# Pairing heads h and h+6 in a score unit, all remaps on SyncE, and a two-queue model of the transfers in the planner

## Chip, cores and metric

The kernel runs on one core of a Trainium2 chip. The metric is the device time of one execution in microseconds (us), given as the median over the runs. The profile is of one execution of its own, and all rows below come from that one.

The core has five instruction streams that matter here. TensorE (PE) multiplies matrices. VectorE (DVE), ScalarE (ACT) and GpSimd (POOL) work on tiles in the on-chip buffers, and GpSimd can also issue transfers. SyncE (SP) computes nothing; it issues transfers, in the order in which the program gives them to it. Each stream works strictly in its own order, so an instruction that waits holds back everything behind it on that engine. The transfers are carried by 16 DMA engines.

## The reference, cut

Talking-heads attention (the heads are mixed before and behind the softmax) feeds two feed-forward blocks.

```python
# q, k, v: [4 batches, 12 heads, 448 positions, 64]; w_pre, w_post: [12, 12]
s = np.matmul(q, k.transpose(0, 1, 3, 2)) / 8
s = np.einsum('bhij,hg->bgij', s, w_pre)
a = np.exp(s - max(s, -1)); a = a / (sum(a, -1) + 1e-9)
a = np.einsum('bhij,hg->bgij', a, w_post)
x = np.matmul(a, v)                      # -> [1792, 768]
h = x @ w_in                             # 768 -> 2048 (weights in float64)
g = where(h >= 1, h, where(h <= -1, 0, (h + 1)**2 / 4))
x = g @ w_out                            # 2048 -> 768
h = x @ w_in2                            # 768 -> 1024
y = h * softmax(h); y = layernorm(y) * g_ln
out = y @ w_out2                         # 1024 -> 768
```

## The kernel before, in words

**Chunks.** Attention is the first third of the program (to about 360 us), and the change is all in it. It runs over 16 chunks: four batches of 448 query positions, each cut into chunks of 110, 110, 110 and 120 positions (`GR` = 11, 11, 11, 12 groups of `R` = 10). Nothing is kept between the chunks but the keys and values of a batch.

**From queries to mixed scores.** For each chunk `load_q` brings the queries of all heads into one of two buffers `qb`. It loads two half tiles; in each the 64 rows are the head's dimensions and a row holds six pieces, one for each head. For each batch `load_k` brings the keys, one tile `kraw` for two heads (ten buffers). A score unit `qk` is four matmuls for two neighbouring heads, 2p and 2p+1, whose queries lie in the lower and the upper 64 partitions; it fills two PSUM tiles of [query position, 448]. `qk_evac` scales and copies each to a tile `s` (12 buffers) on ScalarE; for the odd heads of chunk 0, VectorE does it. Then a transfer, `remap`, moves each `s` tile (110 or 120 rows of 1792 bytes) into the score buffer `sr`. It has two buffers, for even and odd chunks. In `sr` a partition is one head of one position, so that the mixing of heads is a matmul. There are twelve remaps for a chunk. SyncE issues them, but for six of chunk 0 that GpSimd issues.

**From mixed scores to output.** The groups of a chunk are taken two at a time (90 pairs in all). `pre` is eight matmuls that mix the heads, from `sr` with the small weight `wp`. `rmax` (VectorE) finds the row maximum, `expo` (ScalarE) the exponential and its sum, `guard` (GpSimd) and `norm` (VectorE) the reciprocal, `wscale` (GpSimd) multiplies it into the second mixing weight. `post` is 56 small matmuls, `evac` (ScalarE, VectorE) copies into `at`, `av` multiplies by the values, and `store_x` writes the rows of x to memory. The first `pre` of a chunk needs all twelve remaps of the chunk, and the first remap of a chunk needs the last `pre` of the chunk two before it, since that has the same score buffer.

**Near weights.** Beside this, four blocks of the float64 weights of the first feed-forward block are loaded (`e_load`, into `eraw`, one buffer, 0.79 MB each) and taken apart on VectorE, ScalarE and GpSimd (`e_exp` at line 481, `e_pow` at 484 and what follows) into float32, which `e_stash` writes back. They are numbered n = 0 to 3 here; two come from `w_in`, two from `w_out`.

**What sets the order.** A planner (`Order`) places all instructions of all engines before the program is built. Each task has an engine, an estimated duration, its dependences, rings (a pool of n buffers, of which a task takes or frees one) and a priority, which is its place in units of groups with an offset from the table `OFFS`. `emit` always takes the task that can start first, and among those of one engine the one of lowest priority. A transfer is two tasks (`dma`): its issue on an engine, and its flight, which takes a fixed time `xfer` for that kind of load plus 950 ns, whatever else is in flight. A list `gates` holds a load's issue back, in the plan, until the `pre` of a given group. The planner's times only make the order; on the chip each engine waits for the real events.

At the start of the program (`start` in `OFFS`) the first keys and the first queries are loaded in small steps, so that the first two heads can begin early. VectorE clears four rows of the first score buffer (`zero_s`), GpSimd clears small tiles (`zero_w`) and loads the two mixing weights in eight small transfers (`load_w`), from which VectorE forms `wp` and `wk` (`make_w`).

## Time and profile before

| what | value |
|---|---|
| runs before (us) | 1060.23, 1062.01, 1070.85; median 1062.01 |
| span of the profiled execution (us) | 1064.1 |
| TensorE busy | 1016.8 us, 96% of the span, mean granted clock near full |
| VectorE busy | 740.7 us, 70% |
| ScalarE busy | 621.7 us, 58% |
| GpSimd busy | 352.1 us, 33% |
| transfers | 171.41 MB in 101422 packets, mean 161 GB/s |

A row of the timeline reads: start, duration, engine, line and operation, output and inputs with their shape, "x" and the number of instructions in the row, and in brackets how long the engine stood idle before it and what ended that. "SPq" is the issue of transfers on SyncE. In the table by stage, each row is a stretch of the span, and for each engine the busy time and, as "x", the number of instructions. PEld is the loading of weights into TensorE, which lies beside the matmuls. PEclk is the clock that TensorE was granted, as a share of full speed. The last two columns are the mean busy share of the 16 DMA engines and what they moved.

### The profile page before, as it was taken

To read this page: it belongs to the slowest core of one execution; us is meant where nothing else is said; L and a number is where in the kernel's file an instruction comes from. 1 tells how busy PE (TensorE), PEld (TensorE's weight loads), DVE (VectorE), ACT (ScalarE), POOL (GpSimd) and SP (SyncE) were. 2 spreads that over 40 slices of the span, in tenths; PEclk is the share of its full clock that TensorE was granted. 3 is DMA by queue.
4 is the path that set the end of the run, shared out by engine and by line. 5 is a ranking of instruction groups with operands and counts; after the bars stand their busy time and mean duration, and the time that the engine had idled before them with its cause. 6 is when DMAs were issued, how large, how long until landed. Compare 5 with 4: busy or idle time off the path is not lost.

```text
span 1064.1 us, 27355 instructions
## 1 busy us (share of the span) xinstructions
PE 1016.8 (96%) x11053; PEld 836.5 (79%) x11053; DVE 740.7 (70%) x1259; ACT 621.7 (58%) x1329; POOL 352.1 (33%) x475
## 2 busy tenths in 40 slices
PE   6869987999999899999999999999999999999998
PEld 2435655665666589999999999999998878889998
DVE  4535654555556763489897768888887899888782
ACT  3666966778878665633444434343434577686770
POOL 3111321211111341445454555464521245041210
PEclk9999999999999999999999999999999999999999
DMA  8766787477575460242424232423355556697421
GB/s 182 204 176 171 205 264 196 141 218 218 176 219 196 155 204 17 79 139 70 139 99 131 98 118 74 148 92 119 124 183 184 195 179 227 232 332 239 159 79 60
DMA packets 101422, 171.41 MB, mean 161 GB/s; under 512 B 22752, under 2 KB 77888, under 8 KB 101296
## 3 DMA queue, kind: packets, MB, share of 16 engines
q1 hardware_dynamic: 100560, 168.46, 50.6%
q0 software_dynamic: 736, 1.21, 0.6%
q8 instruction: 87, 1.43, 0.6%
q14 instruction: 39, 0.32, 0.1%
HBM read 91.07 MB, written 39.85 MB: 123 GB/s over the span
## 4 chain that ended last, share of the span: by engine, by line
PE 80%; DMA 10%; DVE 4%; ACT 3%; issue 1%; SPq 1%; POOL 1%; ACTq 0%; DVEq 0%
PE ps_h L820 7%; PE ps_o L850 7%; PE ps_h L822 7%; PE ps_o L852 7%; PE ps_h L821 7%; PE ps_o L851 7%; PE ps_pre L340 6%; PE ps_post L376 5%; PE ps_av L427 4%; PE ps_qk L313 4%; DMA sr<-s 4%; PE ps_ot L1184 3%; PE ps_ot L1186 3%; PE ps_ot L1185 3%; PE ps_h L1184 3%; PE ps_h L1186 3%
## 5 line engine op out<-in xcount | busy, mean ns | idle before, releaser
L345 DVE TENSOR_REDUCE nm<-ps_pre 128x1 f32<-128x448 f32 x180 | 105.8, 617 | 50.7 <-PE ps_pre L340 43.0
L850 PE MATMUL ps_o<-g,wout 128*128 128x448 f32 x384 | 139.5, 363 | 0.9 <-DVE x2acc L860 0.9
L852 PE MATMUL ps_o<-g,wout 128*128 128x448 f32 x384 | 139.1, 362 | 0.0
L851 PE MATMUL ps_o<-g,wout 128*128 128x448 f32 x384 | 138.4, 360 | 0.0
L376 PEld LDWEIGHTS ps_post<-wr,p 64*64 64x64 f32 x5040 | 103.1, 136 | 41.2 <-issue 24.7
L350 ACT ACTIVATE p<-ps_pre,nm 128x448 f32<-128x448 f32 x180 | 114.2, 642 | 24.1 <-DVE nm L345 23.9
L842 POOL TENSOR_TENSOR g<-t,g 128x448 fp32r<-128x448 f32 x64 | 83.4, 1303 | 108.5 <-ACT g L838 96.1
L340 PE MATMUL ps_pre<-sr,wp 64*64 64x448 f32 (+1 forms) x720 | 104.8, 575 | 13.6 <-DMA sr<-s 4.0
L313 PE MATMUL ps_qk<-kraw,qb 64*64 64x448 f32 (+2 forms) x768 | 102.8, 568 | 15.1 <-DMA qb<-in_q_dram 5.8
L324 ACT ACTIVATE s<-ps_qk 119x448 f32<-119x448 f32 (+1 forms) x186 | 92.6, 568 | 38.8 <-PE ps_qk L313 24.7
L860 DVE TENSOR_TENSOR x2acc<-ps_o,x2acc 128x448 f32<-128x448 f32 x168 | 100.4, 617 | 19.5 <-PE ps_o L852 18.1
L739 POOL TENSOR_TENSOR m<-m,v 128x768 f32<-128x768 f32 (+1 forms) x48 | 88.6, 1847 | 71.2 <-DVE v L721 56.3
L376 PE MATMUL ps_post<-wr,p 64*64 64x60 f32 x5040 | 104.5, 221 | 4.8 <-issue 2.2
L357 POOL TENSOR_SCALAR nm<-nm 128x2 f32<-128x2 f32 x90 | 19.2, 213 | 235.6 <-ACT p L350 235.5
L826 ACT ACTIVATE t<-ps_h,st 128x448 f32<-128x448 f32 x64 | 40.4, 631 | 69.4 <-PE ps_h L822 67.7
L711 ACT ACTIVATE v<-v,st 128x768 int32<-128x768 int32 (+1 forms) x48 | 42.3, 880 | 64.1 <-DVE v L707 64.0
L852 PEld LDWEIGHTS ps_o<-g,wout 128*128 128x128 f32 x384 | 72.1, 188 | 5.6
L850 PEld LDWEIGHTS ps_o<-g,wout 128*128 128x128 f32 x384 | 72.1, 188 | 5.1 <-DVE x2acc L860 1.3
L340 PEld LDWEIGHTS ps_pre<-sr,wp 64*64 64x64 f32 (+1 forms) x720 | 30.4, 135 | 58.0 <-issue 16.7
L851 PEld LDWEIGHTS ps_o<-g,wout 128*128 128x128 f32 x384 | 71.8, 187 | 5.0
L820 PE MATMUL ps_h<-sr,win 128*128 128x448 f32 x192 | 70.3, 366 | 0.0
L427 PE MATMUL ps_av<-at,vv 128*64 128x240 f32 (+1 forms) x648 | 68.3, 353 | 1.5 <-issue 1.5
(192 smaller groups left out, 2434.1 us busy)
## 6 DMA issues: line engine op xcount, KB each, us to landing
sr<-s SPq DMA_DIRECT2D x138, 192.5 KB
raw<-in_moe_w_out_dram SPq DMA_DIRECT2D x22, 768.0 KB
raw<-in_moe_w_in_dram SPq DMA_DIRECT2D x14, 768.0 KB
sr<-s SPq DMA_DIRECT2D x48, 210.0 KB
xe<-e SPq DMA_DIRECT2D x14, 512.0 KB
el<-xe SPq DMA_DIRECT2D x14, 512.0 KB
raw<-in_moe_w_in_dram SPq DMA_DIRECT2D x12, 512.0 KB
kraw<-in_k_dram SPq DMA_DIRECT2D x24, 224.0 KB
```

Source lines behind the costliest of these rows:

```text
L313: nc.tensor.matmul(out=qk_t[b, c, 2 * p + e][64 * j:at_], lhsT=qb[rows, i % 2, lo:hi], rhs=kraw_t[b, p][rows], start=True, stop=True,)
L324: nc.scalar.activation(out=s[:n], in_=qk_t.pop((b, c, h))[:n], func=AF.Copy, scale=0.125)
L340: nc.tensor.matmul(out=pre_t[t][o:o + 64], lhsT=wp[k_], rhs=sr[i % 2][k_, g, :], start=True, stop=True)
L345: nc.vector.tensor_reduce(nm_t[t // 2][:, 0, t % 2:t % 2 + 1], pre_t[t], axis=AX.X, op=ALU.max, negate=True)
L350: nc.scalar.activation(out=p, in_=pre_t.pop(t), func=AF.Exp, bias=nm[:, 0, e], accum_out=nm[:, 1, e])
L376: nc.tensor.matmul(out=ps[i][64 * j:64 * j + 64, k, :], lhsT=ps_p[e][64 * i:64 * i + 64, x:x + 64], rhs=wr[64 * i:64 * i + 64, e], start=T ...
L427: nc.tensor.matmul(out=ps[0][64 * j:64 * j + 64, a, :2 * w].rearrange("p (e s c) -> p e s c", e=2, c=SEG), lhsT=v_t[b][:, 1 + m, h * D:(h ...
L820: nc.tensor.matmul(out=ps, lhsT=wh, rhs=xh, start=(kk == 0), stop=False)
L850: nc.tensor.matmul(out=ps, lhsT=wh, rhs=g[:, 0], start=(i == 0), stop=False)
L851: nc.tensor.matmul(out=ps, lhsT=wh, rhs=g[:, 1], start=False, stop=False)
L852: nc.tensor.matmul(out=ps, lhsT=wl, rhs=g[:, 0], start=False, stop=(i == 1))
L860: nc.vector.tensor_tensor(out=dst, in0=op.pop((u, m)), in1=dst, op=ALU.add)
```

## The change

- A score unit now holds heads p and p+6 (in `qk`, and in the loads). The lower 64 partitions hold heads 0 to 5, the upper ones heads 6 to 11. So a query load is two transfers of 64 rows, each one piece of 2640 bytes (2880 in a chunk of 120), where each row had six pieces of 440 bytes; and the first query load of the program is no longer split.
- A key load is now for four heads (two units), in two halves of 64 partitions with two pieces each. The bytes are the same, and there are five buffers of double size for ten.
- All remaps are issued by SyncE. The six of chunk 0 that GpSimd issued are gone from there. `zero_s(0)` goes from VectorE to GpSimd.
- In the planner, the flight of a transfer now queues: `give` keeps two "wires", and each kind of load takes time on one or both of them (`XFER`), then `LAND`. A remap takes 88 ns for each group on the first wire alone.
- The query load of chunk 1 is held in the plan until eight remaps of chunk 0 are issued (`hold`), that of chunk 2 until the first `pre`. The near loads move earlier by four groups (`pr - 8` for `pr - 4`).

The diff, cut to these parts (the long lines of the start tuple and of the old chunk loop are left out):

```diff
+   mw=-5, hold=8, q2=0)
...
+BUFS = dict(kraw=5, q=2, vv=2, s=12, sr=2, p=8, st=8, wr=6, x=3, psa=4, psb=4)
...
+LAND = 1300
+XFER = dict(load_k=lambda *a: (1240, 1240), load_q=lambda *a: (1000, 1000), load_v=lambda *a: (1700, 1000),
+            remap=lambda i, b, c, h, e: ((88 if e == 'SP' else 150) * GR[c], 0), e_load=lambda n: (4000, 3000), e_stash=lambda n: (1700, 1000),
+            store_x=lambda *a: (1000, 900))
...
-        d = self.add("DMA", xfer, prio, nothing, deps=[t], use=on, lat=950)
+        d = self.add("DMA", 0, prio, nothing, deps=[t], use=on, lat=LAND)
         d.issue = t
+        d.load = XFER.get(fn.__name__, lambda *a: (xfer, xfer))(*a)
...
+    def give(self, t, latency, avail, wire, done):
+        for o in t.out:
+            o.ready = max(o.ready, t.start + t.dur + latency(t, o))
+            o.left -= 1
+            if not o.left:
+                if o.eng == 'DMA':
+                    wire[:] = [max(w, o.ready) + x if x else w for w, x in zip(wire, o.load)]
+                    o.start = o.ready
+                    o.dur = max(w for w, x in zip(wire, o.load) if x) - o.ready
+                    done.append(o)
+                    for r, k in o.gives:
+                        r.open_[k] -= 1
+                        if not r.open_[k]:
+                            r.back.append(k)
+                    self.give(o, latency, avail, wire, done)
+                else:
+                    avail[o.eng].append(o)
...
-        nc.vector.memset(sr[i][0:pad], 0.0)
+        (nc.vector if i else nc.gpsimd).memset(sr[i][0:pad], 0.0)
...
     def load_k(b, p):
-        t = pl['kraw'].tile([128, S], F32, tag="kraw", name="kraw")
-        nc.sync.dma_start(out=t, in_=k[b, p])
-        kraw_t[b, p] = t
-
-    def load_q(i, b, c, p0, n):
-        m = GR[c] * R
-        qp = q[b, c, :, :H * m].rearrange("d (p e m) -> e d p m", e=2, m=m)
+        t = pl['kraw'].tile([128, 2, S], F32, tag="kraw", name="kraw")
+        heads = k[b].rearrange("p (e d) s -> d (p e) s", e=2)
         for e in range(2):
-            nc.sync.dma_start(
-                out=qb[e * D:(e + 1) * D, i % 2, QPAD + p0 * m:QPAD + (p0 + n) * m].rearrange("d (p m) -> d p m", m=m),
-                in_=qp[e, :, p0:p0 + n],
-            )
+            nc.sync.dma_start(out=t[e * D:(e + 1) * D], in_=heads[:, 6 * e + p:6 * e + p + 2])
+        kraw_t[b, p], kraw_t[b, p + 1] = t[:, 0], t[:, 1]
+
+    def load_q(i, b, c):
+        n = H // 2 * GR[c] * R
+        for e in range(2):
+            nc.sync.dma_start(out=qb[e * D:(e + 1) * D, i % 2, QPAD:QPAD + n], in_=q[b, c, :, e * n:(e + 1) * n])
...
+        for h in (p, p + 6):
...
-        x = od.dma("SP", 450, 2200, pr - 4, e_load, n, new=[r_er])
-        gates.append((x, pr - 4))
+        x = od.dma("SP", 450, 2200, pr - 8, e_load, n, new=[r_er])
+        gates.append((x, pr - 8))
...
-    t_z = add("Pool", 600, -100, zero_w)
-    t_zs = [add("DVE", 5700, -120, zero_s, 0)]
-    t_lw = add("Pool", 8000, P['lw'], load_w, deps=[t_z], lat=2500)
+    t_z = add("Pool", 1700, -1000, zero_w)
+    t_lw = add("Pool", 5000, P['lw'], load_w, deps=[t_z], lat=3500)
     t_w = add("DVE", 300, P['mw'], make_w, deps=[t_lw])
+    t_zs = [add("Pool", 5700, P['lw'] + 1, zero_s, 0)]
...
+        if i:
+            pr = t0 + P['sq'] - 3
+            q0 = od.dma("SP", 1250, 2000, pr, load_q, i, b, c, new=[r_q], deps=held if i == 1 else ())
+            gates.append((q0, pr if i > 2 else P['q2'] if i == 2 else -1))
+        for p in range(H // 2):
+            pr = t0 + P['qk0'] + P['qks'] * 2 * p
+            if c == 0 and p % 2 == 0:
+                kt[b, p // 2] = od.dma("SP", 900, 1240, pr + P['sk'] - 2 if b else -100, load_k, b, p, new=[r_kraw])
+                if b:
+                    gates.append((kt[b, p // 2], pr + P['sk'] - 2))
+                if i == 0 and p == 0:
+                    q0 = od.dma("SP", 1250, 2000, -100, load_q, i, b, c, new=[r_q])
+            a1 = add("PE", 754, pr, qk, i, b, c, p, deps=[q0, kt[b, p // 2]], new=[r_psa, r_psa],
+                     use=[(r_q, i), (r_kraw, b * H // 4 + p // 2)])
+            for e in range(2):
+                h = p + 6 * e
+                en, dur = ("DVE", 550) if i == 0 and e else ("Activation", 470)
+                a2 = add(en, dur, pr + P['qks'] * e, qk_evac, b, c, h, en, deps=[a1], new=[r_s], use=[(r_psa, -1 if e else -2)])
+                rms.append(od.dma("SP", 850, 900, pr + P['qks'] * e, remap, i, b, c, h, "SP", deps=[a2], use=[(r_s, -1)],
+                                  new=[] if rms else [r_sr], join=[r_sr] if rms else []))
+                if i == 0 and len(rms) == P['hold']:
+                    held = [rms[-1].issue]
```

The planner decides the order from these numbers, so here is what it puts where, at three places.

SyncE's queue from the start of the program, before (`kraw` are keys, `qb` queries, `sr<-s` remaps of 11 groups; "x" counts like transfers in a row):

```order
L282 DMA kraw<-in_k_dram 128x448
L289 DMA qb<-in_q_dram 64x110 x2
L282 DMA kraw<-in_k_dram 128x448
L289 DMA qb<-in_q_dram 64x2x110 x2
L282 DMA kraw<-in_k_dram 128x448 x2
L289 DMA qb<-in_q_dram 64x3x110 x2
L282 DMA kraw<-in_k_dram 128x448 x2
L289 DMA qb<-in_q_dram 64x6x110 x2
L329 DMA sr<-s 10x11x448 x6
L289 DMA qb<-in_q_dram 64x6x110 x2
L329 DMA sr<-s 10x11x448 x11
```

And of the change:

```order
L304 DMA kraw<-in_k_dram 64x2x448 x2
L310 DMA qb<-in_q_dram 64x660 x2
L304 DMA kraw<-in_k_dram 64x2x448 x4
L347 DMA sr<-s 10x11x448 x9
L310 DMA qb<-in_q_dram 64x660 x2
L347 DMA sr<-s 10x11x448 x6
L310 DMA qb<-in_q_dram 64x660 x2
L347 DMA sr<-s 10x11x448 x6
L320 DMA vv<-in_v_dram 64x768 x2
L347 DMA sr<-s 10x11x448 x3
```

Six remaps on SyncE stood between the last piece of query load 0 and query load 1, beside six on GpSimd, and the eleven behind that load were of chunk 1. Now nine stand ahead of query load 1, the last three of chunk 0 and three of chunk 1 behind it, and query load 2 comes before the other remaps of chunk 1.

SyncE's queue around the near load n=3, before (`eraw` is that load; remaps of 12 groups are those of chunk 7, those of 11 groups behind it are of chunk 8):

```order
L282 DMA kraw<-in_k_dram 128x448 x4
L329 DMA sr<-s 10x12x448 x6
L282 DMA kraw<-in_k_dram 128x448
L329 DMA sr<-s 10x12x448 x2
L282 DMA kraw<-in_k_dram 128x448
L329 DMA sr<-s 10x12x448 x4
L473 DMA eraw<-in_moe_w_out_dram 128x1536
L289 DMA qb<-in_q_dram 64x6x110 x2
L329 DMA sr<-s 10x11x448 x4
```

And of the change (`xs<-x` is the store of finished rows):

```order
L310 DMA qb<-in_q_dram 64x660 x2
L478 DMA xs<-x 128x2x228
L304 DMA kraw<-in_k_dram 64x2x448 x2
L478 DMA xs<-x 128x2x228
L304 DMA kraw<-in_k_dram 64x2x448 x2
L491 DMA eraw<-in_moe_w_out_dram 128x1536
L347 DMA sr<-s 10x12x448 x6
L304 DMA kraw<-in_k_dram 64x2x448 x2
L347 DMA sr<-s 10x12x448 x6
```

The near load stood behind all twelve remaps of chunk 7 and all six key loads of the next batch; now it stands before those remaps and the last key load.

TensorE's order around the first `pre`, before; the numbers tell tiles apart, four `qk` rows are one unit, and 44 rows of `qk` stand ahead of these, so the first unit here is the twelfth, the last of chunk 1:

```order
L313 MATMUL ps_qk_287<-kraw_169,qb_117 64x448
L313 MATMUL ps_qk_287<-kraw_169,qb_117 55x448
L313 MATMUL ps_qk_288<-kraw_169,qb_117 64x448
L313 MATMUL ps_qk_288<-kraw_169,qb_117 55x448
L340 MATMUL ps_pre_302<-sr_119,wp_115 64x448 x2
L340 MATMUL ps_pre_303<-sr_119,wp_115 64x448 x2
L340 MATMUL ps_pre_311<-sr_119,wp_115 64x448 x2
L340 MATMUL ps_pre_312<-sr_119,wp_115 64x448 x2
L313 MATMUL ps_qk_326<-kraw_129,qb_117 64x448
L313 MATMUL ps_qk_326<-kraw_129,qb_117 55x448
L313 MATMUL ps_qk_327<-kraw_129,qb_117 64x448
L313 MATMUL ps_qk_327<-kraw_129,qb_117 55x448
```

And of the change; 32 rows of `qk` stand ahead of these, so the first unit here is the ninth:

```order
L331 MATMUL ps_qk_244<-kraw_134,qb_117 64x448
L331 MATMUL ps_qk_244<-kraw_134,qb_117 55x448
L331 MATMUL ps_qk_245<-kraw_134,qb_117 64x448
L331 MATMUL ps_qk_245<-kraw_134,qb_117 55x448
L358 MATMUL ps_pre_253<-sr_119,wp_115 64x448 x2
L358 MATMUL ps_pre_254<-sr_119,wp_115 64x448 x2
L331 MATMUL ps_qk_264<-kraw_134,qb_117 64x448
L331 MATMUL ps_qk_264<-kraw_134,qb_117 55x448
L331 MATMUL ps_qk_265<-kraw_134,qb_117 64x448
L331 MATMUL ps_qk_265<-kraw_134,qb_117 55x448
```

All twelve units of chunks 0 and 1 stood before the first `pre`, and chunk 2's first units came behind two of them. Now nine stand before it, three of them of chunk 1, and the other three of chunk 1 come between the next ones.

## Rows read from the trace of the kernel before

**Rows 1.** Table by stage, core 0; PEclk is the granted clock (share).

```profile
core 0: us, PE busy (x) PEld busy (x) DVE busy (x) ACT busy (x) POOL busy (x), PEclk, DMA share, GB/s
0.00:28.20 28.20, 17.46 (x99) 5.50 (x99) 12.94 (x10) 10.14 (x19) 9.69 (x24) 0.94 0.83 181
28.20:46.00 17.80, 14.54 (x308) 7.96 (x309) 9.22 (x20) 13.07 (x35) 2.89 (x10) 0.91 0.79 221
46.00:69.40 23.40, 18.49 (x380) 9.56 (x381) 10.15 (x22) 16.57 (x43) 3.44 (x12) 1.00 0.65 177
69.40:84.00 14.60, 10.30 (x218) 5.92 (x218) 7.07 (x14) 6.63 (x17) 2.53 (x6) 0.88 0.64 171
...
134.00:147.00 13.00, 10.57 (x270) 7.08 (x264) 6.80 (x17) 7.91 (x24) 2.97 (x6) 1.00 0.87 270
...
172.00:186.00 14.00, 7.69 (x174) 5.35 (x174) 4.80 (x13) 5.65 (x16) 2.16 (x5) 0.96 0.84 200
186.00:344.00 158.00, 154.01 (x3683) 98.51 (x3683) 89.44 (x213) 128.08 (x365) 28.61 (x93) 0.99 0.66 193
344.00:376.00 32.00, 27.41 (x707) 19.43 (x703) 25.93 (x54) 22.06 (x56) 10.29 (x18) 0.95 0.58 189
376.00:800.00 424.00, 424.00 (x2247) 396.23 (x2238) 321.46 (x447) 185.12 (x297) 204.53 (x153) 1.00 0.35 113
```

**Rows 2.** Timeline of TensorE: first "pre" of chunks 0, 1, 2.

```profile
28.19 1.76 PE L340 MATMUL ps_pre<-sr,wp 64*64 64x448 f32 x6 [1.90 <-DMA sr<-s]
...
46.00 0.59 PE L340 MATMUL ps_pre<-sr,wp 64*64 64x448 f32 x2 [2.73 <-DMA vv<-in_v_dram]
...
69.41 0.98 PE L340 MATMUL ps_pre<-sr,wp 64*64 64x448 f32 x8 [2.11 <-DMA sr<-s]
```

**Rows 3.** Chain of waits: start, us, what.

```profile
44.32 11.09 DMA sr<-s
...
129.17 4.83 DMA sr<-s
...
172.04 10.97 DMA eraw<-in_moe_w_out_dram
```

**Rows 4.** Timeline, 169 to 187 us, VectorE and TensorE.

```profile
183.04 0.56 DVE L481 TENSOR_SCALAR ev<-eraw 128x768 int32<-128x768 int32 x1 [8.30 <-DMA eraw<-in_moe_w_out_dram]
...
184.66 0.81 PE L418 MATMUL ps_av<-at,vv 64*64 64x120 f32 x14 [4.81 <-ACT ev L484]
```

**Rows 5.** DMA view, 60 to 65 us: packets, MB, share of 16 engines.

```profile
DMA packets 1103, 0.74 MB, mean 148 GB/s; under 512 B 764, under 2 KB 1103, under 8 KB 1103
...
q1 hardware_dynamic: 1103, 0.74, 63.6%
```

**Rows 6.** DMA view, 120 to 125 us.

```profile
q1 hardware_dynamic: 585, 0.97, 60.9%
```

**Rows 7.** Timeline of SyncE's queue: remaps issued, start us, us.

```profile
9.35 7.36 SPq L329 DMA_DIRECT2D sr<-s  x6
...
18.36 14.92 SPq L329 DMA_DIRECT2D sr<-s  x11
...
43.36 15.14 SPq L329 DMA_DIRECT2D sr<-s  x12
...
117.13 10.19 SPq L329 DMA_DIRECT2D sr<-s  x11
...
159.80 5.17 SPq L329 DMA_DIRECT2D sr<-s  x6
```

**Rows 8.** Line 329, the remaps, over the whole span.

```profile
L329 SPq DMA_DIRECT2D sr<-s x186: 755/756/2167, 9.4 to 335.4; - x186
...
DMA to landing us min/median/max: 5.8/8.7/10.0
```

**Rows 9.** Timeline of GpSimd and VectorE, 0 to 16 us.

```profile
0.98 0.83 POOL L251 MEMSET at<- 128x840 f32 x1
...
1.90 4.54 DVE L254 MEMSET sr<- 4x5376 f32 x1 [1.90 <-issue]
```

## The prediction

> **What bounds it now.** I read the table by stage first, with edges where the trace shows a chunk's first "pre" matmul [rows 1]. From 376 us on TensorE has hardly a gap (424.00 of 424 us busy to 800), so whatever attention loses is lost at the end. From 186 to 344 it is 97% busy and runs 3683 instructions in 158 us, 23.3 per us; I use that as its full pace. From 28.2 to 84 it runs only 308 + 380 + 218 = 906, worth 39 us at that pace, in 55.8 us: 17 us are lost. From 172 to 186 it runs 174, worth 7.5 us of 14: 6.5 lost. From 134 to 147 it runs 270, worth 11.6 of 13: 1.4 lost. Before 28.2 it runs 99 "qk" instructions and waits for loads.

> The timeline then says who was late. Each chunk's first "pre" needs all twelve remaps of its chunk, and the waits of TensorE at 28.19 and 69.41 end in a remap, that at 46.00 in the load beside the last one [rows 2]. The chain of waits has a single remap at 11.09 us from issue to landing where it ends at ScalarE [rows 3]. ScalarE works in order, so an evacuation that waits for a buffer still held by such a remap holds the exponentials behind it. The second kind of stall is the near-weight load eraw: it is issued at 172.04 and on the chain for 10.97 us [rows 3], VectorE waits 8.30 us for it, and TensorE's gap of 4.81 us ends with the step of ScalarE behind that [rows 4].

> **The change, part by part.** *Query loads.* In a window that holds one query load, 1103 packets took 63.6% of 16 engines in 5 us, 50.9 engine-us; 764 of them are its 440-byte pieces, the 339 others hold the other 0.40 MB [rows 5]. In a window of remaps alone 585 packets took 60.9%, 48.7 engine-us, about 87 ns for a row of 1792 bytes [rows 6]; scaled by bytes the 339 took 20 engine-us, so a small piece costs 40 ns. A query load is 768 pieces, 1.9 us on each engine; after, 128 rows of 2640 bytes, by bytes 128 ns each: 1.0 us. It saves 0.9 us a chunk. From 186 us on TensorE's 97% hides that; at the start it is inside the sums below.

> *Remaps: what paces them.* SyncE issued eleven back to back in 10.19 us, 0.93 each, where issuing one takes 0.756 [rows 7, 8]. While it did, the engines were 60.9% busy and no other load was queued [rows 6], so the transfers set the pace, with six engines' worth idle. The rows fit a remap that uses ten engines: 110 rows of 87 ns over ten are 0.96 us, over sixteen 0.60. [...] I take the row. So one queue of ten engines, not SyncE, carries the start, and the planner's two classes describe what the trace shows.

> *All remaps of chunk 0 on SyncE.* Six leave GpSimd, whose remaps landed 8.7 us after issue in the median, 10.0 at most [rows 8]; SyncE's issue slot was 1.23 us at that point (six in 7.36) [rows 7]. The first pair of heads now needs 0.80 MB of keys and queries instead of 0.29, at 181 GB/s [rows 1] 2.8 us more, but the later heads no longer wait for pieces; I start the remaps at 9.0, near the present 9.35. Then come nine at 0.95 (17.6), query load 1 (about 1.3 to issue; with 4.83 to land, as on the chain [rows 3], it is there at 23.7), and the last three remaps, issued by 21.8 and landed at 26.6. The three "qk" pairs of chunk 1 that stand before the first "pre" on TensorE fall between 23.7 and then. First "pre": 26.6, against 28.19; at the sum that counts nothing by itself, since chunk 1 waits anyway. Bounds: 22 with remaps at 0.756 and a landing of 2.6, about half; 36.6 with 1.36 each (eleven in 14.92 [rows 7]) and a landing of 10.0 [rows 8].

> *Chunk 1 begins* when its remaps have landed. They start at about 24.5; 12 x 0.95, query load 2 and two value loads (2.6 to issue) end at 38.5, plus 4.83: 43.3, against 46.0.

> *Chunk 2.* Its remaps overwrite the buffer of chunk 0, so they start when chunk 0's "pre" is through, about 41 (43.36 now [rows 7]). They took 15.14 us because ScalarE stood in the way; at 0.95 they take 11.4. The near load n=0 is now between them: 0.79 MB at the stage's 177 GB/s [rows 1], 4.4. With 4.83 to land chunk 2 begins at 61.6, against 69.41. *Chunk 3*: its remaps need 11.4 + 4.83 and two of the six key issues between, some 2 us, so they land near 80. Chunk 2 at full pace takes 5.5 pairs of groups of some 84 instructions (8 "pre", 56 "post", the rest "qk" and "av"), 3.6 us each, and reaches chunk 3 at 81. So of the 5.2 us that the stage from 69.4 to 84 loses (14.6 less 218 instructions' worth) nothing need stay; as ScalarE's order still holds waits for remaps I credit 1.7. With the 7.8 of chunk 2 the start gives 9.5. Its bounds are 0 (order changes alone) and 20 (all 17 us lost, and 3 at the first "pre").

> *Near loads.* n=3 is now issued before chunk 7's twelve remaps instead of behind them, and its first use stands after 72 reductions instead of 76. The first of those remaps left at 159.80 [rows 7], so the issue comes 12.2 us earlier against a use two pairs, 7.2 us, earlier: 5.0 more slack. Its landing had those remaps ahead; alone 0.79 MB at the 200 GB/s of its stage [rows 1] and the 4.83 above are 8.8 us, 2.2 less. That is 7.2 of the 8.30 that VectorE waited; I credit 5.5 of the 6.5 lost. n=2 stands before three value loads instead of behind them, but its use also comes two groups earlier: 1.0 of the 1.4 lost. Bounds 3 and 7.9.

> *At nothing.* The memset of the first score buffer goes to GpSimd: 840 columns took 0.83 us, so 5376 take about 5.3, ahead of the eight small loads of the weights. VectorE forms the weights behind its own memset of 4.54 [rows 9]; that follows its last evacuation of chunk 0, before 17.6 by the steps above, so they are there near 22. The cover to 26.6 is 4.6 us; what goes beyond that is paid at the first "pre". Heads h and h+6 in one unit: the same four matmuls. Key loads: six as before, each the same bytes. From TensorE's row 1649 to 3429 the order is word for word the old one. The end of attention is re-ordered: 32 us with 27.41 busy [rows 1]; I take 0, bounds 3 either way.

> **Sum.** 9.5 + 5.5 + 1.0 = 16 us. The profiled span is 1064.1, 2.1 above the median of 1062.0; 1064.1 - 16 - 2.1 = 1046.0.

> **Rivals.** *The start does not move* (chance 0.20): the ten-engine queue is as full as before and chunk 2 still begins near 69. For it: 48 remaps and the same keys and values must go through; against: from 46 to 84 the engines were 64 to 65% busy over all, with 15.14 us for twelve remaps that elsewhere take 11. Only the near loads pay: 1062 - 6.5 = 1055.5.

> *The held query load* (0.12), the side on which it gets slower. Query load 1 stands behind nine remaps. At 1.36 each and 10.0 to land query load 1 is there at 32.5, chunk 1's remaps run from 33.5 with 12 x 1.36 + 2.6 and 10.0, so chunk 1 begins at 62.4 instead of 46.0: 16.4 lost, 6.5 regained: 1072. For it: rows with 1.36 and 10.0 exist. Against: they come from a queue that six GpSimd remaps and a small-piece query load shared. It decides as soon as chunk 1 begins after 52.5.

> *TensorE's own pace* (0.13): with landings known to the planner nothing of the 17 us stays lost, 20 + 6.5: 1035.5.

> **Numbers.** The forecast has 0.55, with 1039 to 1052 as its own range. 1031 to 1058 takes in the first and last rival (low: 20 + 7.9 + 3) and leaves out the held load and the rest of the tails, 2 in 10. A measurement of this kernel can tell about 1% from no change. Faster by over 1% (below 1051.4): most of the forecast and the third rival, 0.64; within 1%: the first rival and the forecast's upper end, 0.24; slower: 0.12.

> **What would show it.** Right: first "pre" at 25 to 28, first of chunk 1 at 42 to 45, of chunk 2 at 59 to 64; no wait of VectorE for eraw above 2 us; remaps at 0.9 to 1.0 us. Wrong: a first "pre" after 31, chunk 2 after 67, ScalarE still idle for 3 us at remaps, or a gap of more than 8 us near the end of attention.

## The result, and the profile after

The changed kernel took 1053.59 us in the median (1047.64 to 1064.64, 4 runs), against 1064.24 for the kernel before in the same session (4 runs). The ratio is 0.9874, with an interval from 0.9827 to 0.9921: faster by 1.3%. The ratios in this document leave out the runs that took over 1.5% longer than the fastest of the same kernel (here the one of 1064.64), and the plain medians give 0.990 here. A second session, e5 below, gave 0.9946 (0.9899 to 0.9992, 10 runs). The intervals overlap between 0.990 and 0.992, so the gain is near 1%; single runs of either kernel spread over 2% and more. The time lies inside the range that was forecast (1031 to 1058), but outside the forecast's own one (1039 to 1052), and nearer to the first rival's 1055.5 than to 1046. The median of the second session, 1058.05, lies at the upper edge of the range.

The span of the profiled execution fell from 1064.1 to 1055.0 us. These are the lines of the page for the span and the share of the engines:

```profile
span 1055.0 us, 27346 instructions
PE 1007.7 (96%) x11053; PEld 837.5 (79%) x11053; DVE 744.6 (71%) x1258; ACT 622.3 (59%) x1329; POOL 349.1 (33%) x470
DMA packets 91358, 171.41 MB, mean 162 GB/s; under 512 B 10220, under 2 KB 66016, under 8 KB 91232
```

The bytes are the same, with 10,000 packets fewer. TensorE's busy time fell from 1016.8 to 1007.7 us, as much as the span, and its idle time is 47.3 us in both. So a sum of idle time does not tell where the gain lies, and busy time is no measure of work here: further down, 26 matmuls fill one stretch of 3.40 us and 84 the next. The places of the matmuls in time tell it, and the longer waits tell what set them. This is the table by stage of the changed kernel, its edges at the first "pre" of chunks 0, 1 and 2 (the columns are those of [rows 1]):

```profile
0.00:23.20 23.20, 7.58 (x48) 2.68 (x48) 8.49 (x9) 4.54 (x7) 10.58 (x19) 0.87 0.68 177
23.20:27.50 4.30, 4.24 (x24) 2.69 (x28) 0.00 (x0) 1.89 (x4) 0.00 (x0) 0.52 0.29 92
27.50:47.70 20.20, 16.29 (x339) 9.89 (x331) 9.32 (x20) 16.95 (x45) 2.88 (x10) 1.00 0.83 210
47.70:72.40 24.70, 21.42 (x516) 12.97 (x516) 12.91 (x27) 17.94 (x46) 4.30 (x13) 0.93 0.80 207
72.40:120.00 47.60, 43.19 (x998) 26.56 (x1000) 29.33 (x64) 36.55 (x101) 11.92 (x29) 1.00 0.74 212
120.00:186.00 66.00, 59.28 (x1334) 36.68 (x1330) 38.97 (x92) 50.26 (x144) 16.18 (x38) 0.97 0.75 224
186.00:344.00 158.00, 152.00 (x3692) 99.54 (x3688) 88.03 (x210) 125.46 (x356) 25.01 (x89) 1.00 0.66 190
```

From 72 to 186 us TensorE stands idle for 9 to 10% of the time, where I expected its full pace. The timeline of TensorE names what ended its longer waits (start, duration, what, and in brackets the idle time and who ended it):

```profile
23.27 4.65 PE L331 MATMUL ps_qk<-kraw,qb 64*64 64x448 f32 x24 [9.74 <-DMA qb<-in_q_dram]
27.56 1.10 PE L358 MATMUL ps_pre<-sr,wp 64*64 64x448 f32 x8
...
47.70 2.43 PE L358 MATMUL ps_pre<-sr,wp 64*64 64x448 f32 x10 [3.63 <-DMA vv<-in_v_dram]
...
64.07 0.86 PE L394 MATMUL ps_post<-wr,p 64*64 64x60 f32 x44 [0.82 <-issue]
...
69.06 0.93 PE L394 MATMUL ps_post<-wr,p 64*64 64x60 f32 x48 [1.41 <-issue]
...
72.42 1.73 PE L358 MATMUL ps_pre<-sr,wp 64*64 64x448 f32 x16
...
82.94 0.28 PE L394 MATMUL ps_post<-wr,p 64*64 64x60 f32 x3 [1.49 <-issue]
...
90.87 0.98 PE L394 MATMUL ps_post<-wr,p 64*64 64x60 f32 x53 [1.36 <-issue]
...
93.35 0.59 PE L358 MATMUL ps_pre<-sr,wp 64*64 64x448 f32 x2 [0.68 <-DMA eraw<-in_moe_w_in_dram]
...
124.18 0.34 PE L394 MATMUL ps_post<-wr,p 64*64 64x60 f32 x8 [0.91 <-issue]
...
132.55 1.16 PE L394 MATMUL ps_post<-wr,p 64*64 64x60 f32 x49 [2.13 <-issue]
...
178.57 0.46 PE L394 MATMUL ps_post<-wr,p 64*64 64x60 f32 x15 [2.40 <-issue]
...
218.15 0.62 PE L436 MATMUL ps_av<-at,vv 64*64 64x120 f32 x11 [1.77 <-issue]
...
273.06 0.27 PE L394 MATMUL ps_post<-wr,p 64*64 64x60 f32 x2 [1.26 <-issue]
```

The waits of [rows 2] for a remap at 69.41 and of [rows 4] behind the near load are gone. What is new are nine waits that end with "issue", that is, with nothing the profile shows. They sum to 13.6 us. The kernel before has three of them, at 141.02, 175.34 and 225.17, of 4.3 us in all. Eight of the nine stand before a matmul of a "post", the ninth before one of an "av".

To see where the gain arose I compared the start of the k-th matmul of TensorE (counted from 0) in both traces. The count is not always of the same matmul where the order differs, but at the stages' ends it is close. This is worked out from the traces, in us; minus is ahead of the kernel before, and the columns e4 to e12 are experiments of the next section.

```
   k-th   before    after    e5    e6    e7    e4    e8   e10   e12
    100    29.0 us   +1.2  +0.0  +1.2  +0.5  -4.5  -3.6  +2.2  -2.7
    800    70.3      -3.8  -4.0  -2.2  -7.5 -12.3 -11.4  -6.7 -11.9
   1800   120.6      -3.9  -3.0  +3.1  -4.2  -3.9  -6.3  -2.7 -10.0
   3400   201.1      -8.1  -6.7  -5.5  -3.5  -4.6  -8.2  -6.7 -12.1
   5600   292.8      -5.3  -4.9  -6.0  -1.3  -2.3  -4.1  -5.8 -12.7
   6800   344.3      -5.3  -4.9  -5.9  +1.0  -2.4  -4.0  -5.8 -12.7
   7600   384.3      -9.7  -9.3  -7.9  +1.7  -6.6  -8.3  -9.3 -16.3
  11000  1051.2      -9.5  -9.6  -8.5  +1.7  -7.4  -8.7  -9.8 -16.8
```

For the changed kernel: 3.9 us from the start, 4.2 around the last near load, 2.8 given back between 201 and 293 us, 4.4 at the end of attention, and nothing behind it.

### The profile page after: what moved, and what is told of

Read it like the earlier page. It is cut to its first block, busy times and chain, and to the rows that moved or that the text cites. A ratio compares the mean times of both kernels' runs of the same rounds, so it can differ in the third digit from the quotient of the medians.

```text
span 1055.0 us, 27346 instructions
## 1 busy us (share of the span) xinstructions
PE 1007.7 (96%) x11053; PEld 837.5 (79%) x11053; DVE 744.6 (71%) x1258; ACT 622.3 (59%) x1329; POOL 349.1 (33%) x470
## 3 DMA queue, kind: packets, MB, share of 16 engines
q8 instruction: 87, 1.43, 0.6%
## 4 chain that ended last, share of the span: by engine, by line
PE 82%; DMA 7%; DVE 3%; ACT 3%; issue 3%; SPq 0%; POOL 0%; ACTq 0%; DVEq 0%; POOLq 0%
PE ps_h L831 7%; PE ps_o L861 7%; PE ps_h L832 7%; PE ps_o L862 7%; PE ps_o L863 7%; PE ps_h L833 7%; PE ps_pre L358 6%; PE ps_post L394 5%; PE ps_qk L331 5%; PE ps_av L445 5%; PE ps_h L1195 3%; PE ps_h L1197 3%; PE ps_h L1196 3%; PE ps_ot L1196 2%; PE ps_ot L1195 2%
## 5 line engine op out<-in xcount | busy, mean ns | idle before, releaser
L394 PEld LDWEIGHTS ps_post<-wr,p 64*64 64x64 f32 x5040 | 100.5, 135 | 48.0 <-issue 37.4
L750 POOL TENSOR_TENSOR m<-m,v 128x768 f32<-128x768 f32 (+1 forms) x48 | 85.0, 1770 | 82.2 <-DVE v L732 60.9
L358 PE MATMUL ps_pre<-sr,wp 64*64 64x448 f32 (+1 forms) x720 | 100.7, 560 | 9.5 <-DMA vv<-in_v_dram 3.6
L342 ACT ACTIVATE s<-ps_qk 119x448 f32<-119x448 f32 (+1 forms) x186 | 91.0, 570 | 29.2 <-PE ps_qk L331 27.9
L416 DVE COPY at<-ps_post 128x420 f32<-128x420 f32 x94 | 55.8, 597 | 28.9 <-PE ps_post L394 25.5
L831 PE MATMUL ps_h<-xl,win 128*128 128x448 f32 x192 | 69.6, 363 | 0.0
```

The costliest lines, as they stand in the source:

```text
L342: nc.scalar.activation(out=s[:n], in_=qk_t.pop((b, c, h))[:n], func=AF.Copy, scale=0.125)
L358: nc.tensor.matmul(out=pre_t[t][o:o + 64], lhsT=wp[k_], rhs=sr[i % 2][k_, g, :], start=True, stop=True)
L394: nc.tensor.matmul(out=ps[i][64 * j:64 * j + 64, k, :], lhsT=ps_p[e][64 * i:64 * i + 64, x:x + 64], rhs=wr[64 * i:64 * i + 64, e], start=T ...
L750: nc.gpsimd.tensor_tensor(out=m, in0=m, in1=vt.pop(key).bitcast(F32)[:, :n], op=ALU.mult)
L831: nc.tensor.matmul(out=ps, lhsT=wh, rhs=xh, start=(kk == 0), stop=False)
```

## Experiments

Two theories were set against each other. **F (fetch)**: the "issue" waits are waits for TensorE's own program, which is fetched block by block, and they eat what the better order gives. **D (data)**: they belong to late loads or to the planner's order. Beside that, three parts of the change are undone or done alone. The ratios are to the kernel before on the same chip; differences between sessions below about 0.7% decide nothing.

The page of the changed kernel has 87 packets of 16 KB on a queue q8 of the kind "instruction" (1.43 MB, 0.6% of 16 engines). If they bring TensorE's program, they come one for some 257 of its 22370 instructions. So I counted all of TensorE's instructions in the trace, from 0, to each "issue" wait above 0.35 us: the 22106 matmuls and weight loads of the changed kernel and the 264 waits of its sequencer, mostly for semaphores. Matmuls and weight loads alone do not show the grid.

```
after   1473 1729 2241 2497 4034 4290 6338 8129 10690
   rest of the division by 256: 193 193 193 193 194 194 194 193 194
before  4546 6081 8130            rest: 194 193 194
e1      1730 1985 4034 4289 5570 6337 7873 8129 8386 9922 11969   rest: 193 or 194 for all
```

All twelve of the two kernels lie on a grid of 256. I take the packets of 16 KB for the fetches of its blocks: in the fourteen traces of this study 103 of 104 such waits in the first 420 us lie on the grid (the other is one of 0.40 us in e9), and each of the 103 ends 1.2 to 1.8 us after such a packet has landed.

**e1 and e2: the grid moved.**

```diff
...
+    add("PE", 1, -2000, idle_mm, deps=[t_z], new=[r_psa])   # 32 (e1) or 64 (e2) matmuls of zeros, before all else
```

> The changed kernel with 32 small matmuls on zeros at its very start, while TensorE waits for the first loads. They are 128 instructions with their weight loads; nothing else is moved. Theory F (fetch): in the changed kernel TensorE stands for 13.6 us in nine waits that no engine ends, and all nine lie at the same place of a grid of 256 instructions, so they are waits for the next block of its own program; they eat the gain. Moved by half a block, they leave their places in the program: no such wait within 1 us of the nine old instructions, but others elsewhere; their sum may be anywhere from 5 to 18 us and the time moves with it by the difference. Rival D (data): the waits are the tail of late loads or of the planner's order; they stay with the same instructions, and the time stays within 0.3% of the changed kernel's 1053.6.

Measured, e1: ratio 0.9962 (0.9927 to 0.9997). The small matmuls took 7.0 us and the first remap left 2.0 us later (10.27 for 8.29); the first "pre" came at 27.9, as in the changed kernel. Eleven waits, 16.2 us, each on the grid of all instructions, the added 128 included. In the program itself the grid has moved by half a block, and the waits with it: none stands where one of the nine stood. Three of them, from the timeline of e1:

```profile
68.62 3.26 PE L399 MATMUL ps_post<-wr,p 64*64 64x60 f32 x111 [4.85 <-issue]
...
124.42 0.96 PE L336 MATMUL ps_qk<-kraw,qb 64*64 64x448 f32 x5 [0.94 <-issue]
132.26 1.13 PE L399 MATMUL ps_post<-wr,p 64*64 64x60 f32 x33 [2.67 <-issue]
```

Theory D has fallen: the waits go with the count, not with the work.

> The same with 64 small matmuls, 256 instructions, a whole block, as a control: the grid falls on the same instructions of the program as in the changed kernel. Theory F: the waits come back at the changed kernel's nine places or most of them, 10 to 17 us in all, and the time is that of the changed kernel, about 1053, whatever the small matmuls do at the start. Rival D: as e1, no difference between e1 and e2.

Measured, e2: ratio 1.0063 (1.0017 to 1.0109). As a control it failed: the 64 matmuls took 13.8 us in place of the few that I had taken them for, the remaps began at 17.1 for 8.3, and the first "pre" came 8 us later. Its seven waits (10.2 us) lie on the grid as well, but only one, of 3.76 us, is at a block where the changed kernel waits; no more follows from it.

**e3 and e6: the near loads.** e3 takes the earlier near loads out of the changed kernel, e6 puts them alone into the kernel before.

```diff
-        x = od.dma("SP", 450, 2200, pr - 8, e_load, n, new=[r_er])     (e3; e6 the other way)
+        x = od.dma("SP", 450, 2200, pr - 4, e_load, n, new=[r_er])
```

> The changed kernel with the near loads back at four groups ahead for eight (in the plan). Theory N: of the gain, 3.3 us came from the fourth near load (the lead of TensorE over the kernel before grows from 4.8 to 8.1 us there), so VectorE's wait for it comes back at 5 us or more and the time rises by about 3, to 1057. Rival: the other order of the loads carries it, VectorE's wait stays below 2 us and the time stays.

Measured, e3: ratio 0.9950 (0.9902 to 0.9999), not to be told from the changed kernel's 0.9946. Its profiled execution took 1068.9 us, the longest of the ten, so only one thing is read from it: VectorE's first step on a near block (line 499, four instructions) has no wait for the load in the list of what ended its idle time. The last of the four stands later there, at 186.3 us, where the changed kernel has it at 163.69. As far as this one trace goes, theory N has fallen for the changed kernel: without the earlier load it does not wait either.

> The kernel before with one part of the change alone, the near loads eight groups ahead for four. Theory N: VectorE's wait of 8.3 us for the fourth near load falls below 4 and the time falls by 3 to 6 us (ratio 0.994 to 0.997). Rival: the same transfer engines only serve another load later, and nothing is won; ratio 1.000.

Measured, e6: ratio 0.9995 (0.9949 to 1.0041). The mechanism is seen, in the row of VectorE that answers to [rows 4]: the wait is 0.23 us where it was 8.30.

```profile
162.72 0.56 DVE L481 TENSOR_SCALAR ev<-eraw 128x768 int32<-128x768 int32 x1 [0.23 <-DMA eraw<-in_moe_w_out_dram]
```

In its trace the stretch from the 1800th to the 3400th matmul became 8.6 us shorter, but its start was 3.1 us longer, with a wait of 4.50 on the grid at 46.98. So either the earlier load or the rest of the change takes the wait away, each in one trace, and over ten runs the load alone is worth nothing that can be measured.

**e4: the hold undone.**

```diff
-            q0 = od.dma("SP", 1250, 2000, pr, load_q, i, b, c, new=[r_q], deps=held if i == 1 else ())
+            q0 = od.dma("SP", 1250, 2000, pr, load_q, i, b, c, new=[r_q])
```

> The changed kernel with the query load of chunk 1 not held back behind remaps; it is issued with the first loads. Theory H (the hold costs): TensorE's wait of 9.7 us before 23.3 us falls below 3, chunk 1's scores are formed in it, and the time falls by 2 to 4 us. Rival: the load takes the transfer engines from the keys and the remaps of chunk 0, the first "pre" moves from 27.6 to beyond 30 and chunk 1 begins no earlier than 47; the time stays or rises by up to 3.

Measured: ratio 0.9909 (0.9867 to 0.9952). The start does what theory H says, and more: the wait of 9.74 us is gone, the first "pre" is at 23.72, chunk 1 begins at 40.91. But then the grid takes it. The timeline of e4 on TensorE:

```profile
23.72 6.51 PE L358 MATMUL ps_pre<-sr,wp 64*64 64x448 f32 x32 [2.26 <-DMA sr<-s]
...
40.91 0.59 PE L358 MATMUL ps_pre<-sr,wp 64*64 64x448 f32 x2 [1.10 <-DMA qb<-in_q_dram]
...
65.37 1.55 PE L394 MATMUL ps_post<-wr,p 64*64 64x60 f32 x48 [5.98 <-issue]
...
84.10 0.37 PE L394 MATMUL ps_post<-wr,p 64*64 64x60 f32 x3 [2.82 <-issue]
```

At the 800th matmul it was 12.3 us ahead, at the 1800th 3.9, as the changed kernel. Its ratio lies between the two of the changed kernel, so its time is not to be told from them. Behind the long wait the granted clock was at 0.50 of full speed. Two windows of e4, the first from the last 1.8 us of the wait on (columns as in [rows 1]):

```profile
63.60:73.90 10.30, 7.74 (x92) 4.25 (x96) 3.51 (x5) 3.26 (x9) 1.81 (x1) 0.50 0.67 182
73.90:84.10 10.20, 7.38 (x166) 4.11 (x158) 4.77 (x12) 6.33 (x18) 1.73 (x6) 1.00 0.81 218
```

**e5: the changed kernel again.** No edit.

> The changed kernel as it is, once more, to see what of its waits comes back in another execution. Theory F (fetch): the fetch of a block waits behind whatever loads are in flight, so the waits without a releaser stand at the grid of 256 again but not all at the same blocks; in all 8 to 18 us. Rival D: the same nine waits, each within 0.5 us. The ratio to the kernel before should lie between 0.982 and 0.996 by either.

Measured: ratio 0.9946 (0.9899 to 0.9992). Nine waits on the grid, 12.2 us; seven are at blocks where the first trace has one, six of these within 0.8 us of its size. Those of 0.82 at 64 and 0.91 at 124 us are not there, but one of 2.43 at 138 and one of 0.37 at 174 are. So most of them belong to this kernel's order, and some come and go.

**e7: the planner's old picture of the transfers.**

```diff
-        d = self.add("DMA", 0, prio, nothing, deps=[t], use=on, lat=LAND)
-        d.load = XFER.get(fn.__name__, lambda *a: (xfer, xfer))(*a)
+        d = self.add("DMA", xfer, prio, nothing, deps=[t], use=on, lat=950)
...
-                if o.eng == 'DMA':
+                if False:
```

> The changed kernel with the planner's old model of the flights: all transfers on one line, one after the other, with the old durations. All else (pairs of heads h and h+6, remaps on SyncE, earlier near loads, the hold) is kept. Theory P (the plan carries it): at least half of the gain goes, ratio 0.993 or more, since the order of the remaps and evacuations at the start falls back. Rival: the loads and the near loads carry it, and the ratio stays at 0.987 to 0.991.

Measured: ratio 1.0038 (0.9999 to 1.0076); all of the gain is gone, with every other part of the change in place. Its start is as good as the changed kernel's (4.2 us ahead at the 1800th matmul), against what I expected; what it loses is behind that. Against the changed kernel these are 4.9 us between the 1800th and the 3400th matmul, 2.3 between the 5600th and the 6800th and 5.1 at the end of attention. The near blocks are waited for again, as the timeline of VectorE in e7 shows:

```profile
134.60 0.56 DVE L498 TENSOR_SCALAR ev<-eraw 128x768 int32<-128x768 int32 x1 [3.70 <-DMA eraw<-in_moe_w_out_dram]
...
161.45 0.56 DVE L498 TENSOR_SCALAR ev<-eraw 128x768 int32<-128x768 int32 x1 [3.90 <-DMA eraw<-in_moe_w_out_dram]
```

**e8: no hold, and the bulk loads spread.**

```diff
-            q0 = ..., deps=held if i == 1 else ())
+            q0 = ...)
-                pr = t0 + P['sv'] + m          # values
+                pr = t0 + 0.6 + 1.5 * m
-   wd0=19.858, wds=17.513                      # near loads
+   wd0=18, wds=22.7
```

> The changed kernel without the hold on the query load of chunk 1, and with the near loads and the value loads placed among the remaps of different chunks, so that they do not leave SyncE back to back. Theory F: less is in flight when a block is fetched, the waits without a releaser fall to 4 to 9 us from 13.6, and with 4 us from the start the time is 6 to 10 us below the changed kernel's (ratio to before about 0.980). Rival: the fetch waits do not depend on bunched loads, they stay at 10 us or more, and the ratio is that of the kernel without the hold, 0.991.

Measured: ratio 0.9973 (0.9932 to 1.0014). The waits on the grid fell from the 15.6 us of e4 to 7.6, as theory F says. But the time did not fall as it says, and other waits grew from 16.5 to 24.4 us. In the list of TensorE's costliest lines of e8 (busy us, mean ns, then idle us before them and what ended it), "pre" waits 15.6 us where it waited 10.0 in e4, for remaps and the loads beside them:

```profile
L358 PE MATMUL ps_pre<-sr,wp 64*64 64x448 f32 x720 | 106.1, 581 | 15.6 <-DMA sr<-s 6.1 <-DMA vv<-in_v_dram 3.0 <-DMA kraw<-in_k_dram 2.1
```

That loads among the remaps delay them is my reading of this row. In the two traces e8 is not behind e4 (8.7 us ahead of the kernel before for 7.4), and the intervals of the two ratios overlap, so why the time did not fall stays open.

**e9: more loads.** Seven loads of a near block, which nothing uses, at groups 96, 106 and so on.

```diff
...
+    for j in range(7):
+        x = od.dma("SP", 450, 2200, 96 + 10 * j, e_more, new=[r_er])
+        gates.append((x, 96 + 10 * j))
```

> The changed kernel with seven more loads of 0.79 MB that nothing uses, one for every ten groups from group 96 on (about 225 to 330 us), where the changed kernel has only two waits at the grid (1.8 and 1.3 us). They go into the near loads' buffer, which is free by then. Theory F with its cause (the fetch of a block waits behind bulk loads): between 215 and 345 us the waits at the grid rise from 3.0 us to over 6, at other blocks than before, and TensorE's place at 330 us falls back by 4 to 10 us. Rival: the fetch has its own way to memory, the two waits stay at about 3 us, and only waits for remaps (named as such in the trace) can grow.

Measured, one execution: 1080.1 us. Between 215 and 345 us the waits on the grid are 7.0 us where they were 3.0, at other blocks than before; the two old ones, at 218 and 273, are not among them. They are these, from the timeline of e9:

```profile
306.93 0.59 PE L358 MATMUL ps_pre<-sr,wp 60*64 60x448 f32 x1 [1.15 <-issue]
...
315.42 0.39 PE L394 MATMUL ps_post<-wr,p 64*64 64x60 f32 x11 [3.83 <-issue]
...
330.87 0.75 PE L394 MATMUL ps_post<-wr,p 64*64 64x60 f32 x36 [2.00 <-issue]
```

Against the changed kernel TensorE's place was 4.3 us behind at 215 us, ahead of the first added load, and 19.4 behind at 330: it fell back by 15 us, more than the 4 to 10 that I gave. A wait for keys (3.26 at 251 us) comes on top, and slower matmuls behind the wait of 3.83: the eight of the "pre" at 316.57 took 1.90 us, where eight at 322.75 took 1.14. This agrees with theory F and its cause, but it does not show the cause: it is one execution, and in the same stretch the other traces, without added loads, have from 0 to 5.0 us of such waits (5.0 in e1).

**e10: loads in 13 parts.**

```diff
-            nc.sync.dma_start(out=v_t[b][:, m], in_=rows[128 * (m - 1):128 * m])
+            for lo, hi in ((0, 117), (117, 128)):
+                nc.sync.dma_start(out=v_t[b][lo:hi, m], in_=rows[128 * (m - 1) + lo:128 * (m - 1) + hi])
     (near loads alike; keys, queries and the values' half tiles in 52 and 12 rows)
```

> The changed kernel with its key, query, value and near loads cut so that their row counts are 117 and 11, or 52 and 12, in place of 128 and 64. [...]

Measured: ratio 0.9960 (0.9922 to 0.9997). The waits on the grid are four, 5.6 us, where the two traces of the changed kernel have 13.6 and 12.2. I had two forecasts: waits under 4 us with a ratio of 0.985 or less, or 8 us or more with 0.995 to 1.005. The waits lie between the two and the ratio in the second; both rested on an estimate of which engines carry a load and the fetch, which no run shows. The runs lie closer together, 1054.2 to 1060.6, where e5's, on another chip, lay between 1047.8 and 1068.1. Why the waits are fewer is not shown by it: smaller loads alone could do it. No row of the trace tells engines apart, so which engines carry the fetch stays open. The parts in which a load lands can be counted: by the updates of its semaphore (beside one at its issue where there are fewer than 16) a load of 117 or 52 rows lands in 13 parts here, one of 12 rows in 12, one of 11 in 11, a remap in 10, and in the changed kernel a load of 64 or 128 rows in 16. The time is not to be told from e5's.

**e11: the blocks as they are.**

```diff
-WORDS = dict(qk=16, pre=16, post=128, av=32)      BLOCK, FETCH, AHEAD, SWITCH = 256, 4800, 32, 120
+WORDS = dict(qk=16, pre=16, post=112, av=32)      BLOCK, FETCH, AHEAD, SWITCH = 256, 4800, 63, 120
```

> The changed kernel with the planner's picture of the program blocks set right: it counts 128 instructions for a "post", the trace has 112, and the first boundary lies 31 instructions earlier than it thinks. Nothing else is changed; the order moves by it. Theory F: the plan now sees the waits where they fall, but does not steer around them; waits at the grid 8 to 16 us, ratio 0.985 to 1.000. If the planner's picture was what caused the waits (rival), they fall below 6 us and the ratio to 0.980.

Measured: ratio 0.9960 (0.9920 to 1.0001), ten waits on the grid, 14.2 us. The planner's picture of the blocks was wrong, and setting it right gives nothing that can be measured, as expected of a plan that sees the waits and does not steer around them.

**e12: no hold, and loads in 13 parts.** The edits of e4 and e10.

> The two parts that gave something, together in the changed kernel: the query load of chunk 1 is not held (the first "pre" came 4 us earlier without the hold), and the loads are cut into 117 and 11, or 52 and 12 rows (the waits at the grid fell from 13.6 and 12.2 us to 5.6). If the two add up, TensorE is 4 us ahead of the kernel before at the first "pre" and keeps more than that to 120 us, the waits at the grid stay under 8 us, and the ratio to before is 0.983 to 0.990. Rival: what is won at the start is lost again behind it, as it was without the hold alone, since chunk 2 cannot begin before the buffer of chunk 0 is free; the ratio is that of the cut loads alone, 0.991 to 0.998.

Measured: 1052.49 us in the median, ratio 0.9891 (0.9850 to 0.9932), with runs from 1049.4 to 1058.4. This is the best version of the study over eight runs or more, though its interval overlaps with both of the changed kernel's, so that it is faster than that one is not shown. The profiled execution had a span of 1047.6 us, with three waits on the grid, 4.8 us, and the lead of 10.0 us at the 1800th matmul is kept to the end. The first "pre" is 2.75 us ahead of the kernel before, not 4. From its timeline, the first "pre" and the largest of the three:

```profile
25.44 6.31 PE L362 MATMUL ps_pre<-sr,wp 64*64 64x448 f32 x32 [1.49 <-DMA sr<-s]
...
62.27 0.97 PE L398 MATMUL ps_post<-wr,p 64*64 64x60 f32 x50 [2.23 <-issue]
```

## Why the prediction was right, and where it was not

The direction, the stages and the wide range were right. The sum was 16 us, and the trace gives 9 to 10. That the time fell into the range is in part luck: the start gave 3.9 us for 9.5, and 4.4 us came from the end of attention, which I had put at 0. One term failed at three places, the landing of a transfer in 4.83 us. Term by term:

**The first "pre"** came at 27.56, forecast 26.6. Nine remaps took 9.51 us, 1.06 each, and the held query load landed 5.27 us after its issue, against 0.95 and 4.83 in the working. This term held. That ten engines carry a remap was worked out from [rows 6] and [rows 7]; the trace does not tell engines apart and shows only that a remap lands in 10 parts. SyncE's queue in the changed kernel ("x" counts the transfers of a row):

```profile
8.29 9.51 SPq L347 DMA_DIRECT2D sr<-s  x9
17.86 1.43 SPq L310 DMA_DIRECT2D qb<-in_q_dram  x2
19.39 8.74 SPq L347 DMA_DIRECT2D sr<-s  x6
...
36.56 2.59 SPq L347 DMA_DIRECT2D sr<-s  x3
```

**Chunk 1** began at 47.70, forecast 43.3. The step that failed is the landing: the last remap was issued by 39.15, close to the 38.5 of the working, but landed 8.2 us behind that, not 4.83. Query load 3 and three value loads were issued behind it, and I had priced the landing by a row without such neighbours.

A landing can be read from the trace: the updates of a transfer's semaphore are its parts, and the last one is the landing. This table is worked out so; it has the landing of the last remap of a chunk and, behind the stroke, the start of the chunk's first "pre", in us.

```
           chunk 0         chunk 1         chunk 2         chunk 3
before     27.84 / 28.19   45.59 / 46.00   68.91 / 69.41   96.22 / 96.55
forecast           26.6            43.3            61.6    80    / 81
after      26.22 / 27.56   47.35 / 47.70   69.87 / 72.42   92.95 / 93.35
e5         25.35 / 26.36   47.11 / 47.46   70.34 / 73.19   93.88 / 94.28
e4         23.38 / 23.72   40.67 / 40.91   65.12 / 70.69   86.86 / 93.36
e12        25.31 / 25.44   40.97 / 41.06   64.45 / 67.41   87.35 / 87.44
```

**Chunk 2** was to begin at 61.6 and began at 72.42, beyond the 67 that the prediction gave as a sign of being wrong. Its remaps landed 1.0 us later than before, at 69.87. They were issued from 44.17 to 59.21, forecast 41 to 56.8, and the last landed 10.7 us behind that, not 4.83. With that many transfers under way SyncE is paced by landings too: eight of the twelve issues follow within 0.1 us on the landing of the transfer eight before. The row of 4.83 is from 129 us on; [rows 3] had 11.09 for this stretch, and that was the nearer row. TensorE does not wait at 72.42, since the plan puts other work ahead: it ran 516 matmuls from 47.70 to 72.40, where it ran 380 in the 23.4 us of [rows 1].

**Chunk 3** is where the start gave its 3.9 us (3.0 in e5, forecast 9.5): its remaps landed 3.3 us earlier than before, and in both kernels its "pre" starts 0.3 to 0.4 us behind them. The wait at 93.35 names another load, but it ends as far behind the last remap as the wait of chunk 1 does.

So the four waits on the grid between 64 and 91 us, 5.1 us in all, are not what held chunk 3 back in the changed kernel, since TensorE still waits for remaps behind them; whether these would have landed earlier without the four waits is not shown. Where remaps land earlier, the grid does hold TensorE back: in e4 chunks 2 and 3 begin 5.6 and 6.5 us behind their landings. In e12, with fewer waits on the grid, chunk 3 begins 0.1 us behind its landing, 5.9 us ahead of the changed kernel.

"At full pace" failed as well. I had taken 23.3 matmuls per us for TensorE's full pace and did not ask whether its program arrives at that pace. By [rows 1] that is 46.6 matmuls and weight loads per us, so 256 of them in 5.5 us. In the changed kernel's trace a fetch landed 3.0 us in the mean after TensorE entered the block before, and TensorE went on 1.4 to 1.7 us after the landing at each of the nine waits: 4.6 in the mean, close to 5.5, with a tail beyond it. In the kernel before the tail is hardly shorter (10 of 55 fetches landed more than 4 us after TensorE entered a block, 12 of 56 in the changed kernel), but only three of them made TensorE wait. I take it that its other waits hid the rest.

**The near loads** gave 4.2 us (3.7 in e5) for 6.5. VectorE's wait is gone, as forecast (the load was issued 18.5 us earlier, at 153.54):

```profile
163.69 0.70 DVE L499 TENSOR_SCALAR ev<-eraw 128x768 int32<-128x768 int32 x1
```

But 5.4 us of waits on the grid (124.18, 132.55, 178.57) stand in that stretch for 3.6 before. Why the wait went is also not what I wrote: by the traces of e3 and e6 the earlier issue is enough, and is not needed. What the row gave, 6.5 us lost for a wait of 4.81, fits now: the granted clock was at 0.50 behind it. Two windows of the kernel before, behind that wait and after it:

```profile
185.00:188.40 3.40, 3.40 (x26) 1.41 (x23) 2.97 (x6) 2.53 (x8) 1.60 (x3) 0.50 0.65 210
188.40:191.80 3.40, 3.40 (x84) 2.20 (x76) 1.77 (x3) 2.26 (x7) 1.70 (x2) 1.00 0.58 200
```

And two of the changed kernel, behind its wait of 2.13 us on the grid:

```profile
133.20:136.60 3.40, 3.40 (x41) 1.65 (x37) 1.70 (x4) 2.63 (x6) 1.41 (x3) 0.50 0.56 176
136.60:140.00 3.40, 3.40 (x97) 2.16 (x92) 2.52 (x5) 2.08 (x7) 0.05 (x1) 1.00 0.62 195
```

TensorE is busy in all four, at half the level in the first of each pair; by an estimate from these rows half of 3.4 us, 1.7, is lost on top of the wait. Not every wait has it: behind that of 2.40 us at 178.57 the clock stayed at 1.00.

**At nothing**: the stretch from 201 to 293 us, whose order is almost unchanged, cost 2.8 us, nearly all of it two waits on the grid (1.77 at 218.15 and 1.26 at 273.06). **The end of attention** gave 4.4 us for a forecast of 0 and bounds of 3: a wait for exponentials that the kernel before has at 355.44, and the low clock behind it (0.51 in the mean from 355.70 to 359.10), are not there in the new order: the changed kernel's clock is at 1.00 from 136.6 us to the end of attention. From the timeline of the kernel before:

```profile
355.44 2.38 PE L340 MATMUL ps_pre<-sr,wp 64*64 64x448 f32 x8 [2.94 <-ACT p L350]
```

Of the rivals, the first ("the start does not move") was right about the remaps of chunk 2, which still land near 69, and its 1055.5 is nearer to the measured time than 1046.0; but chunk 3 and the end of attention gave what it did not have. The held query load does not lose the time that this rival feared: it keeps TensorE waiting for 9.74 us, and chunk 1 began 1.7 us later than before, far from the 52.5 from which it decides. But it has a price: without it the remaps of chunks 2 and 3 land 4.8 and 6.1 us earlier (e4). TensorE's own pace was the right question with the wrong answer: with 13.6 us of waits on the grid the program does not arrive fast enough for the 1035.5 that this rival promised.

One sentence of the part on the kernel before is wrong. It says that the old planner took a fixed flight time whatever else is in flight. In fact it put all flights one after the other on a single line, which e7 brings back; the change makes two lines of it, with other durations. No number of the prediction rests on it. One price of the prediction was too high: a packet of 440 bytes took 31 ns in the mean in the window of [rows 5], not 40. No term of the sum uses it.

What stays open: which of the bulk loads' features delays a fetch (bytes in flight, packet size, or the engine that they use), what makes a remap of chunk 2 take 9 us to land where one of chunk 0 takes 5.5 (medians of the changed kernel), and how much of the 0.7% between the two sessions of the changed kernel is chip and how much is chance.

## What to carry to other kernels

Where an engine runs hundreds of short instructions, look at the waits that the profile ends with "issue" and count all its instructions between them, the sequencer's waits on semaphores too. Here they lie on a grid of 256 and end 1.2 to 1.8 us after a packet of 16 KB on the instruction queue, from which I take it that TensorE waits for its own program; a better data order can run into that next, as e4 did with a wait of 5.98 us. Price a landing by a row with the same neighbours: 4.83 us stood for 8 to 11 here. Look at the granted clock behind the long waits of TensorE and price it: here it was 0.50 behind waits of 4.81 and 2.13 us, and 1.00 behind one of 2.40. A planner's model of the transfers can carry a whole gain, as e7 shows, though no instruction differs in kind.

## What the runs showed of the hardware

```profile
DMA packets 440, 1.46 MB, mean 260 GB/s; under 512 B 56, under 2 KB 118, under 8 KB 440
...
q1 hardware_dynamic: 440, 1.46, 100.2%
```

The same view of 129.8 to 131 us has one, of 16 KB, and TensorE goes on at 132.55:

```profile
DMA packets 164, 0.48 MB, mean 400 GB/s; under 512 B 18, under 2 KB 18, under 8 KB 163
...
q1 hardware_dynamic: 163, 0.46, 98.4%
q8 instruction: 1, 0.02, 5.3%
```

Over the fourteen traces of this study (747 fetches in the first 360 us) I sorted the fetches by what SyncE had issued in the 6 us before TensorE entered a block, and took the time from there to the start of the next block's fetch. Where it had issued remaps alone or nothing, this was 1.4 us in the mean, and over 3 us for 8% of 229; with up to 1.2 MB of other transfers 2.0 us, and 21% of 427; with more 2.7 us, and 38% of 91. This is a count over traces, not an experiment; e8, e10 and e12, with loads spread or cut smaller, had fewer waits (7.6, 5.6 and 4.8 us for 12.2 to 15.6), and e9, with more loads, had more.
